# The first batch's token products wait for their own weights alone

## The chip, the cores and the metric

One Trainium2 chip, one core. The time is device microseconds of one execution. The kernel before takes 833.06 us (median of 3 runs, 832.63 to 834.16).

## The reference

Four batches, 576 tokens, 8 heads of 64. Three stages follow each other:

```
attention:  scores = q k^T / 8; keep a row's 32 largest; softmax; times v
gate:       x2 = (sigmoid(conv(x)) * (x @ w_val)) @ w_out
mixer:      theta = x2 @ w_theta;  zr, zi = x2 cos(theta), x2 sin(theta)
            y[t] = sum_s w_tok_r[t,s] zr[s] + w_tok_i[t,s] zi[s];  u = x2 + y
            out = u + max(u @ w_ch, 0)
```

A batch's gate and mixer need all heads of that batch's attention. Nothing passes from one batch to another. The result is float32 throughout.

## The kernel before

**Attention.** The scores' rows are cut into 144 tiles of 128 rows (36 a batch). A loop runs one iteration per tile, and in it each engine gets the pieces of several tiles at different stages: TensorE the scores of a tile three ahead (`ps`, L558 and L559), ScalarE their eviction (L572), VectorE the search for the 32 largest (L594 to L621) and the mask (L674), TensorE the transposes of the masked tile (`pt`, L687), ScalarE their eviction (L706), and at the end of a group of tiles TensorE the product with v (`px`, L778). In this text, tile k's *step* is the stretch from VectorE's mask of tile k to that of tile k+1; VectorE, ScalarE and the others take their queues strictly as the program lays them out, so a step's length is the pace of the whole loop.

**Gate and mixer** are two generators per batch, `front(b)` and `back(b)`, in the list `jobs`. In each iteration `work` draws from the first generator until a budget of about 4150 ns (less what attention's own TensorE work takes) is spent. A generator that yields "sync" ends the drawing for that iteration. These are waits of the program that writes the instructions, not of the chip: what they hold back is laid into a later iteration. So a "sync" sets where in each engine's queue the instructions stand.

`front(b)` lays the products with w_val (`pval`), w_out (`px2t`) and w_theta (`pth`), then sine and cosine (ScalarE, L202, which loads another table and the exponential's table again), and VectorE's products `z` (L986). `back(b)` lays

- the token products `py` (L1127): 4 chunks of channels by 2 halves of tokens (256 and 320 columns), each of 9 matmuls, 4 on `z_0` (the first 256 tokens) and 5 on `z_1` (the rest). VectorE adds a finished one to x2 (L1106, `y_out`);
- the channel products `ph` (L529) of u, which is split into a high and a low part (`U`: ScalarE L411, VectorE L415), with w_ch split likewise (`want`, `hi_-1`, `lo_-1`); VectorE adds them (L1158);
- the turned output `po` (L1180), ScalarE's copy (L1171) and the store.

**Weights** come as raw 64-bit words and are made into float32 by `cvt`, piece by piece, one piece begun every second iteration, in the order conv, val, out, theta, tok, ch. Each piece takes two ScalarE, three VectorE and one GpSimd instruction (L329, L332, L340, L341, L335, L354). `lacking[name]` counts what is still missing. `back(b)` begins when nothing is missing any more (L1114). `want(b, "ch", m)` (L466) splits w_ch up to chunk m; it is called from `y_out` after the second and fourth token product of the first half (L1110), and it also sends the parts to DRAM on SyncE's queue, for later batches. For batches 1 to 3 it does nothing in `back`, and nothing is lacking by then.

PE's queue is put in order by a list scheduler when the program is built; VectorE's and ScalarE's are as the loop writes them.

Of the kernel before, what the change touches and what calls it, by code (L numbers as in the profile page):

```python
# [90 lines left out]
def mixer(ctx, tc, qT, kT, vt, w_val, conv_t, w_out, w_theta, w_tok, w_ch, out, flag):  # L91
# [99 lines left out]
    taken, lacking = set(), {}  # L191
# [206 lines left out]
    def chunk(b, x, what, c):  # L398
        both = parts_of(b, x, what)
        w = COLS[x][1] - COLS[x][0]  # L400
        return both[:, 0, c, :w], both[:, 1, c, :w]
# [6 lines left out]
    def halve(hi, lo, src, key, also=None):  # L408

        def higher():  # L410
            nc.scalar.copy(hi, src)  # L411
            later.append(lower)

        def lower():
            engine(key).tensor_tensor(lo, src, hi.bitcast(F32), ALU.subtract)  # L415
            if also is not None:
                also()
            if PATIENT and attending[0]:
                later.append(lambda: done.add(key))
            else:  # L420
                done.add(key)

        mid.append(higher)

    def halve_room(b, x, what, src):

        both = parts_of(b, x, what)
        lo, hi = COLS[x]
        for c in range(0, NC, 2):
            halve(both[:, 0, c : c + 2, : hi - lo], both[:, 1, c : c + 2, : hi - lo], src[:, c : c + 2, lo:hi],  # L430
                  (what, b, c, x))
        if what == "L" and x:
            halve(both[:, 0, :, hi - lo :], both[:, 1, :, hi - lo :], src[:, :, NF * P :], (what, b, "last", x))

    def halved(b, x, what):
        return [(what, b, c, x) for c in range(0, NC, 2)] + [(what, b, "last", x)] * (what == "L" and x)
# [7 lines left out]
    def place(k, m):  # L444

        if k < 3 or k % 3 == 2:
            dt = F32R if k < 3 else I32
            both = []
            for t in ("hi", "lo"):
                if (t, m) in (("lo", 0), ("lo", 1)):  # L450
                    both.append(ml.tile([P, DM], dt, tag=f"{t}{m}", name=f"{t}{m}_{k}"))
                    continue
                pair = f"{t}{m - m % 2}{m - m % 2 + 1}"
                if (pair, k) not in places:
                    places[pair, k] = ml.tile([P, 2, DM], dt, tag=pair, name=f"{pair}_{k}")
                both.append(places[pair, k][:, m % 2, :])
            return both
        if (k, 0) not in places:
            names = ("val", "out") if k % 3 == 0 else ("theta", "ch")
            for t in range(2):  # L460
                places[k, t] = cp.tile([P, NC, DM], I32, tag=f"w_{names[t]}", name=f"w{t}_{k}")
        return [places[k, t][:, m, :] for t in range(2)]
# [3 lines left out]
    def want(b, name, last=NC - 1):  # L466

        k = PHASES.index((b, name)) if b else -1
        if k > 2:
            return  # L470
        for m in range(last + 1):
            if (b, name, m) in mats:
                continue
            src = W[name][:, m, :] if name == "theta" else W[name][:, :, m * P : (m + 1) * P]
            both = place(k, m)
            mats[b, name, m] = both
            stored[name, m] = dp.tile([P, 2, DM], I32, name=f"{name}{m}")

            def store(both=both, to=stored[name, m]):
                for t in range(2):  # L480
                    nc.sync.dma_start(to[:, t, :], both[t].bitcast(I32))

            hi, lo = (t if name == "theta" else t.rearrange("p (c w) -> p c w", c=NC) for t in both)
            halve(hi, lo, src, ("w", b, name, m), store)
# [11 lines left out]
    def used(b, name):  # L496

        if b:
            k = PHASES.index((b, name))
            for k in {0: (), 1: (3,), 2: (4, 5)}.get(k, (k + 3,)):  # L500
                bring(k)

    def mat(b, name, m, c):
        return tuple(t[:, c * P : (c + 1) * P] for t in mats[b, name, m])
# [7 lines left out]
    def after(*keys):  # L512
        while not done.issuperset(keys):
            yield "sync"
# [6 lines left out]
    def products(ps, terms):  # L521

        last, w = len(terms) - 1, ps.shape[-1]
        for i, (a, b) in enumerate(terms):
            ways = passes(a, b)
            for k, (x, y) in enumerate(ways):
                n = x.shape[-1]
                for o in range(0, P, n):
                    nc.tensor.matmul(ps[o : o + n], x, y, start=(i + k == 0),  # L529
                                     stop=(i == last and k == len(ways) - 1), skip_group_check=(n < P))  # L530
            owe[0] += w * (1.275 if len(ways) > 1 else 1.675)
            if owe[0] >= GRAIN and i < last:
                yield paid()
# [3 lines left out]
    def paid():  # L537
        ns, owe[0] = owe[0], 0.0
        return ns
# [181 lines left out]
    def close(part):  # L721
# [89 lines left out]
        if hp == NP - 1:  # L811
            jobs.append(front(b, (x,) if split else (0, 1)))
            if x:
                jobs.append(back(b))
# [284 lines left out]
    def back(b):  # L1099
        x2T = ms.pop(b)  # L1100

        def y_out(m, h, ps):
            lo, hi = COLS[h]

            def f():
                nc.vector.tensor_tensor(x2T[:, m, lo:hi], ps, x2T[:, m, lo:hi], ALU.add)  # L1106
                if m == NC - 1 and (h or b == B - 1):
                    for k in (h,) if b == B - 1 else range(2):
                        halve_room(b, k, "U", x2T)
                if not h and m % 2:  # L1110
                    want(b, "ch", m)
            return f

        while any(lacking.values()):  # L1114
            yield "sync"
        if b < B - 1:
            for h, m in [(h, m) for h in range(2) for m in range(NC)]:
# [36 lines left out]
        def h_out(m, h, ps):  # L1154
            lo, hi = COLS[h]

            def f():
                nc.vector.scalar_tensor_tensor(x2T[:, m, lo:hi], ps, 0.0, x2T[:, m, lo:hi], ALU.max, ALU.add)  # L1158
                n = b + 1
                if h and n in THREE:  # L1160
                    if m % 2:
                        want(n, "val", m)
                    if (n * NP + m, 0) in there:
                        split_x(n, m, 0)
                done.add(("o", b, m, h))
            return f
# [8 lines left out]
        def turned(tiles):  # L1175
            for i in tiles:
                w = P if i < NF else REM
                po = ps_m.tile([P, NC, P], F32, tag="m", name=f"po_{b}_{i}")
                for c in range(NC):
                    nc.tensor.transpose(po[:w, c, :], x2T[:, c, i * P : i * P + w], ident)  # L1180
                later.append(store(i, w, po))
                yield 450

        for h, m in [(h, m) for h in range(2) for m in range(NC)]:
            lo, hi = COLS[h]
            yield from after(*halved(b, h, "U"), ("w", b, "ch", m))
            ps = ps_m.tile([P, hi - lo], F32, tag="m", name=f"ph_{b}_{m}_{h}")
            yield from products(ps, [(mat(b, "ch", m, c), chunk(b, h, "U", c)) for c in range(NC)])
            later.append(h_out(m, h, ps))
            if (h, m) == (1, NC - 1):  # L1190
                used(b, "ch")
            yield paid()
            if h and m == 1:
                yield from after(*[("o", b, c, 0) for c in range(NC)])
                yield from turned([0, 1])
# [222 lines left out]
```

## Time and profile before

| | us |
|---|---|
| median of 3 runs | 833.06 |
| the profiled execution | 829.74 |
| its span, first to last instruction | 827.9 |

| engine | busy us | share of the span |
|---|---|---|
| TensorE (PE) | 725.3 | 88% |
| VectorE (DVE) | 669.0 | 81% |
| ScalarE (ACT) | 634.0 | 77% |
| GpSimd (POOL) | 451.7 | 55% |

The mean granted clock of TensorE is 0.958 of full speed. The shares are averages over attention with mixer work beside it (to about 711 us) and the last batch's mixer alone (from there on). How the engines stand in the stretch around the change is read from the rows below.

### The profile page before, as it was taken

How to read it: one execution, taken by the hardware profiler on the slowest of the kernel's cores; microseconds unless marked ns; L12 is line 12 of the kernel's file. 1: busy time of each engine (PE TensorE's matmuls, PEld its weight loads, DVE VectorE, ACT ScalarE, POOL GpSimd, SP SyncE). 2: the span in 40 equal slices, each digit the busy share in tenths (PEclk: the TensorE clock that was granted, in tenths of full speed). 3: DMA queues.
4: the chain of work that ended last, by engine and by line, in shares of the span. 5: the costliest groups of instructions: out<-in, count | busy, mean ns of one | idle time of the engine just before them, and what ended most of it. 6: DMA issues, size and time to landing. Idle time of an engine off the chain costs nothing.

```text
span 827.9 us, 15411 instructions
## 1 busy us (share of the span) xinstructions
PE 725.3 (88%) x4478; PEld 584.6 (71%) x4478; DVE 669.0 (81%) x2708; ACT 634.0 (77%) x1517; POOL 451.7 (55%) x557
## 2 busy tenths in 40 slices
PE   5467799958995799989889989999999899999995
PEld 3346577635754586778778767778988777898895
DVE  5999999879976979799899979989998695363522
ACT  6788999889769768788988988889987785346511
POOL 5976777446644554546687625647896252005500
PEclk9998999979997699989998999999999999999998
DMA  5676776545342225234855543234763200071002
GB/s 151 167 186 168 197 175 171 136 110 139 97 133 47 71 81 145 53 83 135 230 170 160 163 133 86 46 85 126 189 172 109 103 7 10 1 223 39 2 1 62
DMA packets 69985, 94.33 MB, mean 114 GB/s; under 512 B 13315, under 2 KB 36739, under 8 KB 69891
## 3 DMA queue, kind: packets, MB, share of 16 engines
q1 hardware_dynamic: 69568, 92.82, 41.2%
q8 instruction: 38, 0.62, 0.3%
q14 instruction: 59, 0.46, 0.2%
q10 hardware_dynamic: 320, 0.43, 0.2%
HBM read 49.96 MB, written 13.11 MB: 76 GB/s over the span
## 4 chain that ended last, share of the span: by engine, by line
PE 47%; DVE 27%; ACT 15%; POOL 4%; issue 3%; DMA 2%; SPq 1%; ACTq 0%; POOLq 0%; DVEq 0%
PE py L1127 9%; PE px L778 8%; DVE cand L594 5%; PE ph L529 4%; DVE s L674 4%; DVE thrs L621 4%; PE px2t L529 4%; PE pval L529 4%; PE pth L529 4%; PE pt L687 3%; PE py L1146 3%; PE ps L558 3%; ACT n L607 2%; DVE cand L600 2%; DVE gp L843 2%
## 5 line engine op out<-in xcount | busy, mean ns | idle before, releaser
L615 POOL TENSOR_TENSOR y<-s,n 128x576 f32<-128x576 f32 x144 | 188.9, 1312 | 205.0 <-DVE thrs L621 144.0
L594 DVE MAX8 cand<-s 128x8 f32<-128x96 f32 x864 | 210.5, 244 | 0.8 <-ACT s L572 0.6
L674 DVE SCALAR_TENSOR_TENSOR s<-s,thrs,e 128x576 f32<-128x576 f32 x144 | 137.8, 957 | 10.9 <-ACT e L202 10.9
L607 ACT ACTIVATE n<-s,tops 128x576 bf16<-128x576 f32 x144 | 112.1, 778 | 32.3 <-POOL y L615 11.3
L572 ACT ACTIVATE s<-ps 128x256 f32<-128x256 f32 (+1 forms) x288 | 103.7, 406 | 33.5 <-PE ps L691 11.5
L1127 PE MATMUL py<-w_tok,z 128*128 128x256 f32 (+1 forms) x432 | 115.0, 407 | 3.4 <-DVE z L986 3.4
L687 PE MATMUL pt<-ident,s 128*128 128x128 f32 x576 | 95.8, 290 | 25.3 <-ACT pT L706 17.3
L621 DVE MAX8 thrs<-y 128x8 f32<-128x584 f32 x144 | 109.3, 759 | 4.1 <-POOL y L616 3.6
L202 ACT ACTIVATE e<-s,least 128x576 f32<-128x576 f32 x144 | 110.8, 769 | 0.5 <-DVE s L674 0.4
L687 PEld LDWEIGHTS pt<-ident,s 128*128 128x128 f32 x576 | 70.5, 148 | 49.9 <-ACT pT L706 21.9
L558 PE MATMUL ps<-kh_None,q 128*128 128x256 f32 x240 | 93.7, 397 | 5.9 <-ACT s L572 3.9
L1127 PEld LDWEIGHTS py<-w_tok,z 128*128 128x128 f32 x432 | 77.8, 190 | 22.3 <-DVE z L986 5.0
L706 ACT COPY pT<-pt 128x512 f32<-128x512 f32 x128 | 73.2, 572 | 25.8 <-PE pt L687 15.6
L778 PE MATMUL px<-pT,v 128*64 128x256 f32 (+1 forms) x512 | 75.3, 430 | 17.3 <-ACT pT L706 17.3
L598 DVE MAX8 tops<-cand 128x8 f32<-128x48 f32 x432 | 82.8, 192 | 0.1
L559 PE MATMUL ps<-kl_None,q 128*128 128x256 f32 x240 | 72.5, 305 | 0.0
L778 PEld LDWEIGHTS px<-pT,v 128*64 128x64 f32 x512 | 34.1, 142 | 47.2 <-ACT pT L706 19.7
L558 PEld LDWEIGHTS ps<-kh_None,q 128*128 128x128 f32 x240 | 47.4, 198 | 22.2 <-ACT s L572 10.7
L600 DVE MATCH_REPLACE8 cand<-tops,cand 128x48 f32<-128x48 f32 x288 | 55.2, 192 | 0.0
L558 PE MATMUL ps<-kh,q 128*128 128x256 f32 (+1 forms) x80 | 36.0, 458 | 21.4 <-ACT s L572 9.3
L559 PEld LDWEIGHTS ps<-kl_None,q 128*128 128x128 f32 x240 | 48.1, 200 | 2.7 <-issue 0.5
L695 ACT COPY pT<-ps 64x128 f32<-64x128 f32 (+1 forms) x160 | 39.2, 245 | 11.5 <-PE ps L691 5.6
(206 smaller groups left out, 1726.9 us busy)
## 6 DMA issues: line engine op xcount, KB each, us to landing
kh_None<-kh_None SPq DMA_DIRECT2D x48, 144.0 KB, 2.7
kl_None<-kl_None SPq DMA_DIRECT2D x48, 144.0 KB, 2.7
v<-in_vt_dram SPq DMA_DIRECT2D x20, 256.0 KB, 3.3
out_dram<-x2T SPq DMA_DIRECT2D x16, 256.0 KB, 3.0
w<-ch SPq DMA_DIRECT2D x16, 256.0 KB, 4.6
w<-theta SPq DMA_DIRECT2D x16, 256.0 KB, 5.4
raw_hi<-in_w_tok_dram SPq DMA_DIRECT2D x7, 512.0 KB, 4.0
kh<-kh SPq DMA_DIRECT2D x24, 144.0 KB, 2.4
```

Source lines behind the costliest of these rows:

```text
L202: ins = nc.scalar.activation(out, src, func, **more).ins
L529: nc.tensor.matmul(ps[o : o + n], x, y, start=(i + k == 0), stop=(i == last and k == len(ways) - 1), skip_group_check=(n < P))
L558: nc.tensor.matmul(bank[:, :w], q2, kh[:, lo:hi], start=(j == js[0]), stop=False)
L559: nc.tensor.matmul(bank[:, :w], q2, kl[:, lo:hi], start=False, stop=(j == js[-1]))
L594: nc.vector.max(d["cand"][:, k, 8 * x : 8 * x + 8], s_tiles[i][:, x * SUB : (x + 1) * SUB])
L607: nc.scalar.activation(n, s_tiles[i], AF.Sign, bias=d["tops"][:, k, KC - 1 : KC], scale=-(1.0 + 2.0 ** -22), accum_out=acc)
L615: nc.gpsimd.tensor_tensor(y[:, :S], s_tiles[i], d.pop(("n", k)), ALU.mult)
L621: nc.vector.max(thrs[:, N - 1 - i : N - 1 - i + NK], d.pop(("y", k)))
L674: nc.vector.scalar_tensor_tensor(p, p, thr(i), e.exp, ALU.is_ge, ALU.mult, accum_out=part["sums"][:, e.slot : e.slot + 1])
L687: nc.tensor.transpose(e.pt[:, c, :], p[:, c * P : (c + 1) * P], ident)
L778: nc.tensor.matmul(px[d, :], of_v, pT[:, k, :], start=(c == 0), stop=(c == NF), skip_group_check=True)
L1127: nc.tensor.matmul(ps, z[:, m * P : (m + 1) * P], W["tok"][:, w, lo:hi], start=(i + k == 0), stop=(i == NF))
```

## The change

`back(b)` waits only until the token weights are converted. The second and third hunk split w_ch later: `y_out` notes each chunk of the first half in `due`, and calls `want` for all noted ones when its chunk is odd and w_ch is converted; whatever is left over is split before the channel products.

```diff
@@ back(b)
-                if not h and m % 2:
-                    want(b, "ch", m)
+                if not h:
+                    due.append(m)
+                    while due and m % 2 and not lacking["ch"]:
+                        want(b, "ch", due.pop(0))
             return f
 
-        while any(lacking.values()):
+        due = []
+        while lacking["tok"]:
             yield "sync"
@@ before the channel products
+        while lacking["ch"]:
+            yield "sync"
+        while due:
+            want(b, "ch", due.pop(0))
```

What this does to the queues. In the names below, `pt_51` are the transposes of tile 51, `py_0_1_0` is the token product of batch 0, channel chunk 1, token half 0; `z_0_0` and `z_0_1` are batch 0's z of the first 256 tokens and of the rest.

TensorE's queue from the transposes of tile 51 to those of tile 52, before:

```order
L687 MATMUL pt_51_3465<-ident_91,s_51_2911 128x128 x4
L558 MATMUL ps_60_0_3414<-kh1_6_None_3062,q21_88 128x256
L559 MATMUL ps_60_0_3414<-kl1_6_None_3063,q21_88 128x256
L691 MATMUL ps_60_0_3414<-ident_91,s_50_2844 64x128
L558 MATMUL ps_60_256_3418<-kh1_6_None_3062,q21_88 128x320
L559 MATMUL ps_60_256_3418<-kl1_6_None_3063,q21_88 128x320
L687 MATMUL pt_52_3508<-ident_91,s_52_2964 128x128 x4
```

The same place now, with the four matmuls ahead of it:

```order
L1130 MATMUL py_0_0_0_3421<-w_tok_138,z_0_1_3050 128x256 x4
L687 MATMUL pt_51_3470<-ident_91,s_51_2911 128x128 x4
L1130 MATMUL py_0_1_0_3493<-w_tok_138,z_0_0_2006 128x256 x2
L558 MATMUL ps_60_0_3414<-kh1_6_None_3062,q21_88 128x256
L559 MATMUL ps_60_0_3414<-kl1_6_None_3063,q21_88 128x256
L691 MATMUL ps_60_0_3414<-ident_91,s_50_2844 64x128
L558 MATMUL ps_60_256_3418<-kh1_6_None_3062,q21_88 128x320
L559 MATMUL ps_60_256_3418<-kl1_6_None_3063,q21_88 128x320
L1130 MATMUL py_0_1_0_3493<-w_tok_138,z_0_0_2006 128x256 x2
L1130 MATMUL py_0_1_0_3493<-w_tok_138,z_0_1_3050 128x256
L687 MATMUL pt_52_3523<-ident_91,s_52_2964 128x128 x4
L1130 MATMUL py_0_1_0_3493<-w_tok_138,z_0_1_3050 128x256 x2
```

Four token matmuls stand ahead of tile 51's transposes, five between them and tile 52's, two right behind these; before, none. The first four of all stand ahead of tile 50's transposes, and 23 ahead of tile 53's; before, the first one stood behind tile 54's.

TensorE's queue where batch 0's turned output ends, before:

```order
L687 MATMUL pt_76_4975<-ident_91,s_76_4375 128x128 x4
L1180 MATMUL po_0_2_4993<-ident_91,x2T_0_1697 128x128 x4
L1180 MATMUL po_0_3_5005<-ident_91,x2T_0_1697 128x128 x4
L687 MATMUL pt_77_5041<-ident_91,s_77_4424 128x128 x3
L558 MATMUL ps_86_0_4998<-kh1_9_None_4663,q21_88 128x256
L559 MATMUL ps_86_0_4998<-kl1_9_None_4664,q21_88 128x256
L691 MATMUL ps_86_0_4998<-ident_91,s_76_4375 64x128
L558 MATMUL ps_86_256_5002<-kh1_9_None_4663,q21_88 128x320
L559 MATMUL ps_86_256_5002<-kl1_9_None_4664,q21_88 128x320
L687 MATMUL pt_77_5041<-ident_91,s_77_4424 128x128
L1180 MATMUL po_0_4_5066<-ident_91,x2T_0_1697 64x128 x4
L529 MATMUL pval_1_0_0_5131<-X_1_0_4781,hi01_0_4831 128x256 x2
```

Now:

```order
L687 MATMUL pt_72_4801<-ident_91,s_72_4184 128x128 x3
L1183 MATMUL po_0_4_4826<-ident_91,x2T_0_1697 64x128 x4
L558 MATMUL ps_82_0_4831<-kh0_9_None_4536,q20_87 128x256
L559 MATMUL ps_82_0_4831<-kl0_9_None_4537,q20_87 128x256
L691 MATMUL ps_82_0_4831<-ident_91,s_72_4184 64x128
L735 MATMUL ps_82_0_4831<-ident_91,rs_7_1_4725 5x128
L558 MATMUL ps_82_256_4836<-kh0_9_None_4536,q20_87 128x320
L559 MATMUL ps_82_256_4836<-kl0_9_None_4537,q20_87 128x320
L778 MATMUL px_7_1_4839<-pT_7_1_4282,v2_7_0_4532 64x320 x8
L778 MATMUL px_7_1_4839<-pT_7_1_4282,v_last_121 64x320 x2
L687 MATMUL pt_73_4871<-ident_91,s_73_4242 128x128 x4
L558 MATMUL ps_83_0_4886<-kh0_9_None_4536,q20_87 128x256
```

The last turned output `po_0_4` stands with tile 72's transposes and not with tile 77's. The first three `pval` of batch 1 begin behind tile 74's transposes (before, tile 77's) and end, as before, ahead of the fourth's place behind tile 80's. From tile 80's transposes on TensorE's queue, and from tile 82's mask and exponential on VectorE's and ScalarE's, the instructions are the same in the same order in both programs. On GpSimd's queue the four low parts of x's second half for batch 1 (`X_1`, L415) stand one tile earlier, together with the last one of the first half (`X_0`).

VectorE's queue from the mask of tile 59, before:

```order
L674 SCALAR_TENSOR_TENSOR s_59_3396,sums_6_0_3559<-s_59_3396,thrs_127,e_59_3783 128x576
L796 TENSOR_TENSOR xT_5_3536<-px_5_1_3651,rb_5_1_3565 128x320
L415 TENSOR_TENSOR lo0_-1_3799<-w_ch_139,hi01_-1_3798 128x512
L415 TENSOR_TENSOR lo1_-1_3801<-w_ch_139,hi01_-1_3798 128x512
L621 MAX thrs_127<-y_62_3828 128x8
```

Now:

```order
L674 SCALAR_TENSOR_TENSOR s_59_3396,sums_6_0_3583<-s_59_3396,thrs_127,e_59_3807 128x576
L796 TENSOR_TENSOR xT_5_3560<-px_5_1_3676,rb_5_1_3589 128x320
L415 TENSOR_TENSOR lo0_-1_3823<-w_ch_139,hi01_-1_3822 128x512
L415 TENSOR_TENSOR lo1_-1_3825<-w_ch_139,hi01_-1_3822 128x512
L415 TENSOR_TENSOR lo23_-1_3828<-w_ch_139,hi23_-1_3827 128x512 x2
L621 MAX thrs_127<-y_62_3854 128x8
```

The four low parts of w_ch (and on ScalarE the four high parts ahead of them) stand in one place; before, the second pair stood three tiles later.

## Rows read from the trace of the kernel before

**Rows 1.** The page: its first line.
```profile
span 827.9 us, 15411 instructions
```

**Rows 2.** Busy time by stretch, all engines: stretch, its length, busy us (x instructions), granted clock, DMA.
```profile
core 0: us, PE busy (x) PEld busy (x) DVE busy (x) ACT busy (x) POOL busy (x), PEclk, DMA share, GB/s
188.10:206.70 18.60, 15.34 (x88) 10.37 (x86) 18.60 (x90) 17.74 (x46) 12.36 (x15) 0.91 0.56 154
253.90:281.90 28.00, 13.32 (x58) 8.86 (x60) 22.41 (x81) 22.92 (x50) 14.85 (x17) 0.60 0.16 34
259.40:283.20 23.80, 12.51 (x45) 7.89 (x47) 19.80 (x66) 18.75 (x42) 12.70 (x14) 0.50 0.22 46
263.86:279.03 15.17, 8.34 (x28) 5.46 (x28) 15.13 (x47) 11.45 (x28) 6.76 (x8) 0.50 0.16 35
281.90:390.55 108.65, 103.13 (x647) 83.79 (x644) 96.93 (x428) 86.09 (x215) 57.52 (x70) 0.96 0.38 103
281.90:401.95 120.05, 112.00 (x704) 92.11 (x700) 106.98 (x465) 97.41 (x242) 66.32 (x80) 0.95 0.43 116
283.30:300.00 16.70, 16.70 (x109) 13.52 (x106) 13.03 (x68) 12.63 (x33) 7.02 (x10) 1.00 0.37 96
```

**Rows 3.** The same view, line L674 alone: VectorE's masks, two instructions each.
```profile
0.00:253.90 253.90, 44.96 (x100) 0.95 0.57 149
188.10:206.70 18.60, 4.12 (x10) 0.91 0.56 154
281.90:390.55 108.65, 21.76 (x48) 0.96 0.38 103
```

**Rows 4.** Timeline of TensorE: start, us, instruction, [idle before <- what ended it].
```profile
255.70 0.31 PE L559 MATMUL ps<-kl_None,q 128*128 128x320 f32 x1
263.86 1.12 PE L687 MATMUL pt<-ident,s 128*128 128x128 f32 x4 [7.85 <-ACT pT L706]
...
268.41 1.12 PE L687 MATMUL pt<-ident,s 128*128 128x128 f32 x4 [1.84 <-ACT pT L703]
...
279.03 1.12 PE L778 MATMUL px<-pT,v 128*64 128x256 f32 x4 [3.94 <-ACT pT L706]
```

**Rows 5.** Timeline of VectorE, same stretch: the products with cosine and sine.
```profile
264.45 2.48 DVE L986 TENSOR_TENSOR z<-px,z 128x512 f32<-128x512 f32 x4
...
274.04 0.66 DVE L986 TENSOR_TENSOR z<-px,z 128x512 f32<-128x512 f32 x1
```

**Rows 6.** Timeline of ScalarE, same stretch.
```profile
276.98 0.78 ACT L607 ACTIVATE n<-s,tops 128x576 bf16<-128x576 f32 x1 [3.66 <-POOL y L616]
```

**Rows 7.** The chain that ended last, token products: start, us, what, two records a matmul.
```profile
286.42 3.89 PE py L1127 x18
...
343.67 3.23 PE py L1127 x12
```

**Rows 8.** Waits of VectorE from 282 to 402 us: total us, times, longest.
```profile
DVE x2T L1106 <- PE py L1127: 8.1, 4, 3.3
DVE lo_-1_3799 L415 <- ACT hi_-1_3798 L411: 1.7, 1, 1.7
```

**Rows 9.** Timeline of VectorE, 289 to 360 us: additions of token products, pile-up.
```profile
290.34 0.42 DVE L1106 TENSOR_TENSOR x2T<-py,x2T 128x256 f32<-128x256 f32 x1 [1.04 <-PE py L1127]
...
299.48 0.42 DVE L1106 TENSOR_TENSOR x2T<-py,x2T 128x256 f32<-128x256 f32 x1 [2.62 <-PE py L1127]
...
341.79 0.49 DVE L1106 TENSOR_TENSOR x2T<-py,x2T 128x320 f32<-128x320 f32 x1 [3.34 <-PE py L1127]
...
353.62 2.68 DVE L843 SCALAR_TENSOR_TENSOR gp<-xT,w_conv,gp 128x576 f32<-128x576 f32 x2
...
356.30 2.73 DVE L415 TENSOR_TENSOR U<-x2T,U 128x512 fp32r<-128x512 f32 x4
```

**Rows 10.** Timeline of TensorE, 352 to 358 us: the first channel products.
```profile
357.01 0.58 PE L529 MATMUL ph<-U,hi_-1_3798 128*128 128x256 f32 x1 [1.26 <-DVE U L415]
```

**Rows 11.** Timeline of GpSimd, 403 to 406 us.
```profile
403.73 1.70 POOL L415 TENSOR_TENSOR X<-xT,X 128x320 fp32r<-128x320 f32 x2
```

## The prediction

> **What bounds the kernel now.** I read the page first, then the busy time by stretch, then the timelines of the stretch in which the change works, and last VectorE's waits behind it.
>
> The span is 827.9 us [rows 1]. Fifty masks lie ahead of 253.90 us (100 instructions, two a mask) [rows 3], so tile 50's step begins there. Steps 50 to 53 fill 28.00 us, 7.00 each, and in them TensorE is busy for 13.32 us only, at a mean granted clock of 0.60 [rows 2]. This is a hole. ScalarE does batch 0's last sines and cosines with two table loads, and TensorE stands from about 256.0 to 263.86 us because the evicted transposes are late [rows 4]; then VectorE makes `z`, five products up to 274.7 us [rows 5], and is busy for 15.13 of 15.17 us [rows 2]. So the hole belongs to ScalarE and VectorE, not to TensorE: work put on TensorE there costs nothing as long as it is done in time, and its absence shortens nothing.
>
> Behind it lie 24 steps (54 to 77) in 108.65 us [rows 2, 3], 4.53 each, with batch 0's token products, channel products and turned output beside attention. TensorE is busy for 103.13 us of them, VectorE for 96.93: the two share the bound. Where attention runs nearly alone, as in steps 36 to 40, five masks take 18.60 us, 3.72 each, and VectorE is busy all the time [rows 2, 3]. A step without mixer work is thus 0.81 us shorter. From 281.90 to 401.95 us VectorE idles 120.05 - 106.98 = 13.07 us [rows 2]; 8.1 of that it waits for token products, at the head of its queue [rows 8].
>
> **What is moved.** 23 of batch 0's 72 token matmuls stand ahead of tile 53's transposes now, and before none did. One with 256 columns takes 3.89 / 9 = 0.432 us, one with 320 3.23 / 6 = 0.538 (two records a matmul) [rows 7]. So 9.9 us of TensorE's work, out of 36 x 0.432 + 36 x 0.538 = 34.9, go into the hole. The back of batch 0 ends five tiles earlier (72 instead of 77). From tile 80 on nothing can move further ahead, since batch 1's gate waits for its own attention; what is won must be won before.
>
> **Does it fit?** Between 263.86 and 279.03 us TensorE did 8.34 us of its own work, all of it at the clock's low level, 0.50 (1.2 GHz) [rows 2]. The four matmuls on `z_0` ahead of tile 50's transposes run while it would stand. The other 19 come behind the first `z`, at 265 us at the earliest [rows 5]. I take the low level up to tile 51's transposes: four matmuls at 0.864 = 3.5 us from about 266.6, so these begin near 270.0, not at 268.41 [rows 4]. From there TensorE has some 5.6 us of own work (at the low level) and 15 matmuls. At the high level that is 2.8 + 15 x 0.432 = 9.3 us, done at 279.3, just where the product with v begins now (279.03) [rows 4]. The 1.6 us of delay are covered by ScalarE, which stands for 3.66 us before 276.98 [rows 6]. I cost the hole at nothing but VectorE's addition of the first product, 0.42 us [rows 9], which came later before.
> Bounds: all 19 at the high level, and TensorE is early, with no gain since VectorE is full; all 19 at the low level, 16.4 + 8.34 = 24.8 us in 15.17, and it is 9.6 us late.
>
> The clock decides this, and the row shows it at 0.50 for the whole of 259.40 to 283.20 us, with TensorE busy for 12.51 of 23.80, and at 1.00 from 283.30 us on, after it had worked without a pause since 279.03 [rows 2, 4]. The Trainium skill (TensorE: Matmul & The Clock Gate, "What's actually happening") says that the low clock is the default state and that sustained activity releases it. By that rule the added matmuls, which close the pauses, lift the clock inside the hole, and the sum is the one above; by the row alone, which holds no such activity in the hole, it stays low and the case "late" below comes true.
>
> **The sum, in two ways.** First by the pace of steps: 20 steps (54 to 73) keep 4.53 us, since 25.0 us of token products in 20 are about as dense as 34.9 in 24; four (74 to 77), with three `pval` alone, fall to 3.72. 4 x 0.81 = 3.2 us, less 0.42: 2.8.
> Second by VectorE's waits: the two for products of the first half, 1.04 and 2.62 [rows 9], go, as these are done in the hole. In step 70 two conv taps (2.68 us) and the four low parts of u (2.73) pile up, and TensorE waits 1.26 us for the latter [rows 9, 10]; now u is split four tiles earlier, away from the taps. 1.04 + 2.62 + 1.26 - 0.42 = 4.5 us. The long wait of 3.34 for a product of 320 columns stays, as these run beside attention as densely as before.
> Smaller edits: w_ch's four parts are split in one go; VectorE waited 1.7 us for the first pair before [rows 8] and waits in that one place for both now: nothing. The eight stores stand in one row on SyncE's queue ahead of the next head's loads, four of them not there before; they wait for two more low parts, about 0.7 us each by the four of u [rows 9]. The scores that need these loads stand behind tile 62's transposes, three tiles on: nothing. GpSimd's five splits of x stand together; four took 3.4 us [rows 11]; VectorE may wait for one more, 0.85 us.
> I take 4.2 us, nearer the second sum, as VectorE's queue carries the loop's pace, and expect it to be kept to the end, since the order is the same from tile 82 on. Profiled execution: 829.74 - 4.2 = 825.5 us. It ran 3.3 us below the median of the runs, so for the median 833.06 - 4.2 = 828.9.
>
> **Rivals.**
> - *More:* the work done in the hole unloads TensorE so far that VectorE waits no more between 281.90 and 401.95 us, but for the 1.7 us for ScalarE's split of w_ch [rows 8]: 13.07 - 1.7 - 0.42 = 10.9 us, 822.2. For it: TensorE is the busier of the two in steps 54 to 77. Against: the products of 320 columns meet the same density of work as before. With the 1.7 us too it would be 820.4.
> - *Nothing:* VectorE and ScalarE carry steps 54 to 79 whatever TensorE does, or what was won until 73 is given back where batch 1's x is split: GpSimd's five splits hold up VectorE's search, and the gate's first products wait there in both programs. Left: 3.66 of the waits, less 0.42 and less some 2.2 us at these splits (by estimate the 1.26 us that TensorE waited for u's split, and one split of 0.85): 1.1 us, 832.0. For it: VectorE is busy for 96.93 of 108.65 us. Against: the 3.72 us of a step without mixer work.
> - *Late:* the clock stays low in the hole. The token matmuls stand ahead of the transposes in TensorE's queue, which takes them in order; 9.6 us late less the 3.66 that ScalarE can spare, less the 4.2 won later: +1.7, without ScalarE's slack +5.4. The middle, 836.6. It decides from 7.9 us of delay on, that is when some 15 of the 19 run at the low level. For it: 0.50 over the whole hole. Against: the pauses in it are closed.
> - *Not what it says:* that w_ch's conversion ends so soon after the token weights' that nothing moves is excluded by the order, which shows five tiles.
>
> **Chances.** Forecast 0.58 (its own range 825.5 to 831.4, a gain of 1.7 to 7.5), more 0.14, nothing 0.17, late 0.11. What a measurement of this kernel can tell from no change is 0.2%, 1.7 us. Faster by more: the forecast but for a small share, and "more", together 0.72; within: "nothing" and that share, 0.18; slower 0.10. The range that leaves out 2 in 10 goes from 822.0, just below "more", to 832.8, which takes in "nothing" and leaves out "late".
>
> **What would show it.** Token matmuls between 256 and 279 us; granted clock back at 1.00 before 275 us; steps 50 to 53 still about 28 us; tile 54's mask within 1 us of 281.97; the first two waits of VectorE for token products gone, a long one at a 320-column product left; steps 74 to 77 below 4 us; masks from tile 82 to the end in the same distances as before. Wrong it would be if steps 50 to 53 grew by more than 3 us, if steps 54 to 73 took over 4.7 us each, or if the lead at tile 80 were lost later.

## The result and the profile after

The changed kernel takes 822.0 us in the first measurement (median of 4 runs, 821.0 to 824.7) and 823.5 in a second one beside other kernels (6 runs, 821.6 to 825.2). The ratio to the kernel before is 0.988 (95% interval 0.984 to 0.992) and 0.990 (0.988 to 0.993): faster, by 8 to 10 us. The forecast was 828.9, a gain of 4.2. Sign and place were right, and the size was about half of what came. The 822.0 of the first measurement stands on the lower end of the stated range (822.0 to 832.8).

The page of the changed kernel, the span and the busy time of each engine:

```profile
span 819.2 us, 15413 instructions
...
PE 717.9 (88%) x4478; PEld 577.3 (70%) x4478; DVE 667.2 (81%) x2708; ACT 633.8 (77%) x1517; POOL 453.3 (55%) x557
```

The span was 827.9 [rows 1], so 8.7 us went. TensorE's busy time fell by 7.4 us from 725.3 although it does the same products; the mean granted clock is 0.973, before 0.958, so less of them ran at the low level. The change reaches the steps from tile 50 to tile 81. Their two ends are these masks, first before, then now:

```profile
253.95 0.81 DVE L674 SCALAR_TENSOR_TENSOR s<-s,thrs,e 128x576 f32<-128x576 f32 x1
...
411.45 0.80 DVE L674 SCALAR_TENSOR_TENSOR s<-s,thrs,e 128x576 f32<-128x576 f32 x1
```

```profile
253.65 0.81 DVE L674 SCALAR_TENSOR_TENSOR s<-s,thrs,e 128x576 f32<-128x576 f32 x1
...
403.38 0.81 DVE L674 SCALAR_TENSOR_TENSOR s<-s,thrs,e 128x576 f32<-128x576 f32 x1
```

They took 157.50 us and take 149.73, so 7.8 us of the gain stand here; a second trace of the changed kernel has 149.73 as well. Where in them the time went, the stretches tell. Steps 50 to 53, then 54 to 73, 74 to 77 and 78 to 81 of the changed kernel, and behind them the two parts of the hole on either side of the clock's return:

```profile
core 0: us, PE busy (x) PEld busy (x) DVE busy (x) ACT busy (x) POOL busy (x), PEclk, DMA share, GB/s
253.65:282.02 28.37, 20.81 (x118) 16.20 (x116) 22.78 (x82) 22.95 (x50) 14.95 (x17) 0.88 0.18 38
282.02:368.89 86.87, 82.44 (x539) 65.68 (x535) 83.56 (x363) 76.13 (x191) 50.17 (x61) 1.00 0.48 127
368.89:383.03 14.14, 10.49 (x86) 9.74 (x82) 14.14 (x67) 13.78 (x38) 9.84 (x12) 1.00 0.81 235
383.03:403.35 20.32, 13.71 (x88) 10.28 (x89) 16.38 (x73) 15.65 (x39) 14.21 (x23) 0.83 0.40 100
```

```profile
259.96:266.78 6.82, 3.17 (x11) 2.66 (x12) 3.71 (x8) 6.79 (x14) 2.75 (x3) 0.50 0.64 136
266.78:282.02 15.24, 13.86 (x81) 10.49 (x80) 15.20 (x56) 9.88 (x25) 8.52 (x10) 1.00 0.04 8
```

The same steps of the kernel before (54 to 73, 74 to 77, 78 to 81), cut at its own masks:

```profile
281.97:373.75 91.78, 86.26 (x521) 69.04 (x518) 80.21 (x356) 71.70 (x178) 47.03 (x58) 0.96 0.37 98
373.75:390.63 16.88, 16.88 (x129) 14.82 (x128) 16.74 (x74) 14.40 (x38) 10.50 (x13) 1.00 0.43 131
390.63:411.41 20.78, 17.04 (x121) 14.96 (x120) 18.49 (x75) 19.41 (x48) 16.41 (x25) 0.92 0.93 245
```

Steps 50 to 53 are as long as before (28.37 against 28.00 [rows 2]), with 7.5 us more of TensorE in them. Steps 54 to 73 lose 4.9 us and 74 to 77 lose 2.7. Over these 24, VectorE was busy for 96.93 of 108.65 us [rows 2]; now it is for 83.56 + 14.14 = 97.70 of 101.01. The same work stands closer together, and VectorE is busy for 97%. In all, from mask 50 on: +0.35 in the hole, -4.9, -2.7, -0.5 in steps 78 to 81, -0.6 to the end, and the rest (0.3) was there before the change's place. The 0.6 are not the change's: they go in steps 110 to 130, and the two traces of one later version differ by as much there (29.09 and 29.71 us in steps 110 to 115).

TensorE's timeline in the hole, the added matmuls among the work of before [rows 4]:

```profile
255.55 1.89 PE L1130 MATMUL py<-w_tok,z 128*128 128x256 f32 x8
263.56 1.12 PE L687 MATMUL pt<-ident,s 128*128 128x128 f32 x4 [6.12 <-ACT pT L706]
...
266.07 2.25 PE L1130 MATMUL py<-w_tok,z 128*128 128x256 f32 x8
268.15 0.62 PE L687 MATMUL pt<-ident,s 128*128 128x128 f32 x4
...
274.47 0.70 PE L1130 MATMUL py<-w_tok,z 128*128 128x256 f32 x2 [1.33 <-DVE z L986]
...
275.75 3.18 PE L1130 MATMUL py<-w_tok,z 128*128 128x256 f32 x14
278.87 0.65 PE L778 MATMUL px<-pT,v 128*64 128x256 f32 x4
```

Transposes took 1.12 us at 263.56 and 0.62 at 268.15: the clock came back between them. VectorE's waits from 282 to 403 us (total, times, longest), which answer to [rows 8]:

```profile
DVE gp L843 <- POOL gp L835: 3.9, 1, 3.9
DVE lo_-1_3823 L415 <- ACT hi_-1_3822 L411: 1.7, 1, 1.7
DVE x2T L1106 <- PE py L1130: 1.0, 1, 1.0
DVE xT L796 <- ACT rb L757: 0.6, 1, 0.6
```

Of the 8.1 us of waits for token products 1.0 is left. The wait of 3.9 us for GpSimd was 1.3 in the kernel before:

```profile
DVE gp L843 <- POOL gp L835: 1.3, 1, 1.3
```

### The profile page after: what moved, and what is told of

Read it like the earlier page. It is cut to its first block, busy times and chain, and to the rows that moved or that the text cites. A ratio compares the mean times of both kernels' runs of the same rounds, so it can differ in the third digit from the quotient of the medians.

```text
span 819.2 us, 15413 instructions
## 1 busy us (share of the span) xinstructions
PE 717.9 (88%) x4478; PEld 577.3 (70%) x4478; DVE 667.2 (81%) x2708; ACT 633.8 (77%) x1517; POOL 453.3 (55%) x557
## 4 chain that ended last, share of the span: by engine, by line
DVE 40%; PE 39%; ACT 9%; POOL 7%; issue 2%; DMA 2%; SPq 0%; ACTq 0%; POOLq 0%; DVEq 0%
DVE cand L594 8%; PE py L1130 7%; DVE s L674 7%; DVE thrs L621 6%; PE px L778 6%; PE px2t L529 4%; PE pval L529 4%; PE pth L529 4%; DVE cand L600 3%; PE ph L529 3%; DVE tops L598 3%; PE py L1149 3%; PE pt L687 3%; DVE gp L843 3%; PE ps L558 2%
## 5 line engine op out<-in xcount | busy, mean ns | idle before, releaser
L674 DVE SCALAR_TENSOR_TENSOR s<-s,thrs,e 128x576 f32<-128x576 f32 x144 | 138.0, 959 | 10.9 <-ACT e L202 10.9
L558 PE MATMUL ps<-kh_None,q 128*128 128x256 f32 x240 | 91.5, 388 | 6.3 <-ACT s L572 3.0
```

Source lines behind the costliest of these rows:

```text
L558: nc.tensor.matmul(bank[:, :w], q2, kh[:, lo:hi], start=(j == js[0]), stop=False)
L674: nc.vector.scalar_tensor_tensor(p, p, thr(i), e.exp, ALU.is_ge, ALU.mult, accum_out=part["sums"][:, e.slot : e.slot + 1])
```

## The experiments

All are timed against the kernel before on their own chip. Three theories: LOAD, what TensorE does in the hole it doesn't do in steps 54 to 77, whose bound it was; CLOCK, the clock's early return helps behind the hole; PILE-UP, VectorE's and ScalarE's pieces of batch 0 stand at better places.

The times scatter by some us within each kernel. Between the masks of tile 50 and tile 82 the traces are far steadier (the two of the changed kernel agree to 0.01 us; most others have one trace), so that stretch is given beside the times; "by the trace" means it.

| trace | us from tile 50's mask to tile 82's | against before |
|---|---|---|
| before | 157.50 | |
| changed kernel, two traces | 149.73, 149.73 | -7.8 |
| nine matmuls ahead | 155.36 | -2.1 |
| hole filled | 155.98 | -1.5 |
| w_ch split in one place | 157.87 | +0.4 |
| twenty left out | 152.53 | -5.0 |
| load put back | 155.81 | -1.7 |
| left out and filled | 153.18 | -4.3 |
| one matmul less | 152.51 | -5.0 |
| u split one tile later | 151.17 | -6.3 |
| splits of x parted, two traces | 147.75, 147.74 | -9.8 |
| two chunks at a time, on top | 148.27 | -9.2 |

**Nine matmuls ahead instead of 23** (against the changed kernel):

```diff
-        while lacking["tok"]:
+        while lacking["tok"] or lacking["ch"] > 1:
```

> The changed kernel, but batch 0's token products start only when the token weights are there and at most one piece of w_ch is missing. 9 token matmuls stand ahead of tile 53's transposes instead of 23, and batch 0's turned output ends with tile 76's transposes, not 72's (before: 0, and 77's). Theory LOAD (TensorE was the bound in steps 54 to 77, the hole is free, so what leaves that stretch is gained nearly one to one: 8 of 9.9 us): 9 x 0.432 = 3.9 us moved, gain about 3.2 us, 829.7. Theory CLOCK (the gain is the clock that stays up): the pauses are half closed, gain of 1 to 4 us. Theory PILE-UP (the gain is that conv taps and u's split, and w_ch's two splits, no longer stand in each other's way): the order behind is nearly that of before, gain under 1 us.

829.2 us, ratio 0.9965 (0.994 to 0.999): 2.9 us gained, by the trace 2.1. Nine matmuls are 3.9 us of TensorE's work, so 0.75 us were won for each us moved, by the trace 0.55. LOAD and CLOCK both allowed this; PILE-UP's "under 1 us" missed.

**The hole filled, nothing moved** (against the kernel before; 23 matmuls whose sums nobody reads):

```diff
+        if b == 0:
+            while lacking["tok"]:
+                yield "sync"
+            ...  # 23 token matmuls on z_0 and z_1 into a spare tile
         while any(lacking.values()):
```

> The kernel before, with 23 token matmuls added in the hole (the same as those that the change moves there, into scratch tiles that nobody reads); batch 0's own 72 stay behind tile 53's transposes. LOAD: no gain, 0 to 0.5 us slower, 833. CLOCK: the clock is back before 270 us as in the changed kernel, and the product with v at 279 us runs at the high level: 2.1 us faster there, more if the lead holds, 829 to 831. PILE-UP: no gain.

829.2 us, 0.997 (0.994 to 1.000): some 2.5 us. Its hole is 28.00 us long, so filling it costs nothing, and the clock there is that of the changed kernel (0.88). The hole and steps 54 to 77:

```profile
254.40:282.40 28.00, 20.42 (x114) 16.31 (x114) 22.39 (x81) 22.94 (x50) 14.83 (x17) 0.88 0.16 35
282.40:390.00 107.60, 102.37 (x644) 83.22 (x641) 96.51 (x429) 87.13 (x216) 57.00 (x70) 0.97 0.39 105
```

The filling alone is thus worth about a quarter of the gain by the middle of its interval (0.3 to 4.7 us), and a fifth by the trace (1.5 of 7.8). That is what CLOCK expected; LOAD's "no gain" missed. TensorE stays the busier one in steps 54 to 77 (102.37 of 107.60).

**w_ch split in one place** (the kernel before; at `m == 3`, as the change does):

```diff
-                if not h and m % 2:
+                if not h and m == NC - 1:
```

> The kernel before, with w_ch's four parts split in one place, after the fourth token product of the first half; the start of the token products is as before. LOAD and CLOCK: 0 within 0.5 us. PILE-UP: one stop instead of two for VectorE (1.7 and 0.6 us of waits before), 1 to 2 us faster, 831 to 832.

832.2 us, 1.0011 (0.999 to 1.003): nothing, and by the trace 0.4 us more. This part of PILE-UP falls.

**Twenty matmuls left out, none moved into the hole** (the kernel before):

```diff
-                for x in range(2):
+                for x in range(1 if b == 0 and h == 0 else 2):
...  # the sum of such a product ends with z_0's last matmul
```

> The kernel before, leaving out 20 of batch 0's token matmuls (those of the first half of tokens on the later 320 tokens' z); the start is as before, nothing runs in the hole, 52 matmuls stand in steps 54 to 63, and from the channel products on the order is that of the changed kernel. LOAD: as fast as the changed kernel within 1.5 us, 821 to 824, since only the dense stretch counts. CLOCK: the hole keeps its low clock to 283 us, so 2 us or more slower than the changed kernel. If work in the hole has a price of its own, this one is faster than the changed kernel by that price.

827.2 us, 0.993 (0.991 to 0.995): 5.7 us for 8.6 us of TensorE's work, with the clock low through the hole and beyond it:

```profile
258.40:285.70 27.30, 14.37 (x53) 8.59 (x53) 21.69 (x80) 22.05 (x49) 14.69 (x17) 0.50 0.25 54
```

That is slower than LOAD had it (821 to 824) and as CLOCK had it (2 us or more behind the changed kernel). Less load without CLOCK, but with the earlier places that batch 0's later pieces get by it, carries more than half by the middle of its interval (3.8 to 7.7 us), and 5.0 of 7.8 us by the trace.

**The changed kernel again.** No edit.

> The changed kernel itself, on the chip of the three kernels beside it, since its time so far comes from 4 runs (821.0 to 824.7). Both theories: 820.5 to 824.5 us against 832.1 for the kernel before. Above 826 the gain would be nearer the 4.2 us forecast than the 10 measured, and the question of the second half would be gone.

823.5 us, told above. The gain stands.

**The load put back** (against the changed kernel; 16 matmuls run twice, 8.6 us; the other engines' queues are the same, row for row):

```diff
-                            nc.tensor.matmul(ps, z[:, m * P : (m + 1) * P], W["tok"][:, w, lo:hi],
-                                             start=(i + k == 0), stop=(i == NF))
+                            for r in range(2 if b == 0 and h == 1 and x == 0 else 1):
+                                nc.tensor.matmul(ps, z[:, m * P : (m + 1) * P], W["tok"][:, w, lo:hi],
+                                                 start=(i + k + r == 0), stop=(i == NF))
```

> The changed kernel with the work that it took off steps 54 to 77 put back on TensorE alone: the four matmuls on z_0 of each of batch 0's four 320-column products run twice (16 more matmuls of 0.54 us, 8.6 us, against 20 x 0.43 = 8.6 taken off); the output isn't the reference's. VectorE, ScalarE and GpSimd have the same instructions in the same order, and the hole keeps its 23 token matmuls. Theory LOAD (TensorE was the bound of these steps): VectorE waits for the 320-column products again, some 5.7 us of the gain go, 826 to 829 us. Rival ORDER (what counts is when VectorE and the others get batch 0's pieces, and the clock's return in the hole): under 2 us more than the changed kernel, 822 to 824.

830.1 us, 0.997 (0.996 to 0.999): 6.6 us more than the changed kernel on the same chip (5.8 by the ratios, 6.1 by the trace), somewhat more than LOAD had it, and ORDER falls. What is left of the gain, with the clock's return, the new places and 1.3 us of load not put back, is 1.7 us by the trace. VectorE's waits from 282 to 403 us show where:

```profile
DVE xT L796 <- ACT rb L757: 4.1, 1, 4.1
DVE gp L843 <- POOL gp L835: 3.9, 1, 3.9
DVE x2T L1106 <- PE py L1131: 3.4, 3, 1.9
```

The waits for token products are back (3.4), and one of 4.1 us for ScalarE's copy of what TensorE makes in its queue behind them. These 16 matmuls stand in steps 59 to 65 and the moved ones stood from step 55 on, so 6.1 may be an upper end; no run shows it.

**Twenty left out and the hole filled**: the two edits above together.

```diff
+        ...  # the 23 matmuls in the hole
-                for x in range(2):
+                for x in range(1 if b == 0 and h == 0 else 2):
```

> The kernel before without 20 of batch 0's token matmuls and with 23 matmuls in the hole whose sums nobody reads: the two edits measured apart (5.0 and 2.9 us by the medians), now together; the output isn't the reference's. Theory SUM (the change is these two effects, which add): 823 to 825.5 us, near the changed kernel. Rival OVERLAP (a faster clock in the hole helps only because TensorE is late behind it, so with the load gone it buys nothing): 826.5 to 828.5, as with the matmuls left out alone.

827.2 us, 0.994 (0.992 to 0.996): no faster than without the filling, as OVERLAP had it. But the two runs differ by more than the filling. On ScalarE's queue w_ch's and u's high parts and the first pieces of batch 1's x and w_val stand later here. From tile 54's mask to tile 64's this run takes 42.99 us, the one without the filling 45.49: the filling wins 2.5 us with the load gone, and they are lost behind, where the queues differ. So it isn't shown that the clock is no second term beside LOAD. By the trace 3.4 us of the gain had no owner here. Beside the 3.9 us for GpSimd that the changed kernel has too, VectorE waits longest for the last 320-column product. TensorE's timeline there, then VectorE's:

```profile
327.30 3.40 PE L1150 MATMUL py<-w_tok,z 128*128 128x320 f32 x12
...
331.39 2.37 PE L778 MATMUL px<-pT,v 128*64 128x320 f32 x16
333.59 0.71 PE L778 MATMUL px<-pT,v_last 128*64 128x320 f32 x4
334.23 0.66 PE L687 MATMUL pt<-ident,s 128*128 128x128 f32 x4
334.72 0.70 PE L1150 MATMUL py<-w_tok,z 128*128 128x320 f32 x2
```

```profile
335.46 0.49 DVE L1106 TENSOR_TENSOR x2T<-py,x2T 128x320 f32<-128x320 f32 x1 [3.70 <-PE py L1150]
```

The last matmul (two records) stands behind the product with v and a tile's transposes; in the changed kernel the whole product stands ahead of them.

**One matmul less**, this one, on top of the two edits above:

```diff
+                            last = (b, h, m) == (0, 1, NC - 1)
+                            if not (last and i == NF):
                                 nc.tensor.matmul(...
```

> As the matmuls left out and the hole filled, and besides without the last matmul of batch 0's last 320-column product, so 21 are left out. In the run before, this one matmul stood behind the 20 of the product with v and a tile's transposes in TensorE's queue, and VectorE's addition waited 3.70 us for it at the head of its own. Theory PLACE (what the changed kernel has beyond the lower load is that this product ends ahead of the product with v): the wait falls to some 0.5 us and the time by 2.5 to 3.2 us, to 824 to 825 us, near the changed kernel. Rival LOAD ALONE (one matmul less is 0.54 us of TensorE, and VectorE waits elsewhere instead): 826.5 to 827.2 us.

826.2 us, 0.993 (0.991 to 0.995), the same within its interval and 0.7 us less by the trace; between PLACE and LOAD ALONE, nearer the latter. PLACE falls in this form: the wait for the product is gone, and in the next step VectorE waits 3.03 us for ScalarE's high parts of u. ScalarE's timeline shows why, first here, then in the changed kernel:

```profile
332.67 0.77 ACT L202 ACTIVATE e<-s,least 128x576 f32<-128x576 f32 x1
335.46 0.59 ACT L706 COPY pT<-pt 128x512 f32<-128x512 f32 x1 [2.02 <-PE pt L687]
...
338.12 2.40 ACT L411 CAST U<-x2T 128x512 fp32r<-128x512 f32 x4
```

```profile
330.98 0.77 ACT L202 ACTIVATE e<-s,least 128x576 f32<-128x576 f32 x1
331.65 2.38 ACT L411 CAST U<-x2T 128x512 fp32r<-128x512 f32 x4
333.94 0.57 ACT L706 COPY pT<-pt 128x512 f32<-128x512 f32 x1
```

The changed kernel has u's split one tile earlier in ScalarE's queue, beside the product with v, where ScalarE stands for 2.02 us in the other.

**u split one tile later** (the changed kernel; ScalarE's queue around it is then that of the run above):

```diff
-                if m == NC - 1 and (h or b == B - 1):
+                if m == NC - 1 and (h and b or b == B - 1):
...
+        if b == 0:
+            yield "sync"
+            for k in range(2):
+                later.append(lambda k=k: halve_room(b, k, "U", x2T))
         while lacking["ch"]:
```

> The changed kernel with batch 0's split of u one tile later: on ScalarE the four high parts (L411, 2.4 us) now stand behind the eviction of the transposes that TensorE makes after a group's product with v (3.1 us of TensorE), where the two runs with matmuls left out have them; in the changed kernel they stand ahead of that eviction. All arithmetic and TensorE's load stay. The run with one matmul less moved VectorE's wait from the product to these high parts (3.03 us) and won nothing, so Theory SLOT: what the changed kernel has beyond the lower load is that ScalarE splits u beside the product with v instead of standing, and VectorE's search goes on; one tile later it loses 2 to 3.5 us, 825 to 826.7 against 823.1 (10 runs of the changed kernel). Rival ELSEWHERE (the rest of the gain comes from other steps, as the move of w_ch's four parts behind a lighter load): within 1 us, 822 to 824.

824.3 us, 0.990 (0.988 to 0.993): 1.2 above the 10 runs of the changed kernel by medians, and nothing by the ratios. By the trace it is 1.4 us. That is between the two expectations. The first pieces of batch 1's x and w_val stand later on ScalarE's queue too, so not all of it need be u's. The stall of ScalarE is there, but VectorE waits only 0.90 us for u:

```profile
334.39 0.59 ACT L706 COPY pT<-pt 128x512 f32<-128x512 f32 x1 [2.02 <-PE pt L687]
```

SLOT is worth up to some 1.4 us; in the size expected of it, it fell.

**GpSimd's five splits of x parted** (against the changed kernel, in batch 1's gate):

```diff
+                if b == 1 and (x, c) == (0, NC - 1):
+                    yield "sync"
```

> The changed kernel with a yield between GpSimd's split of X_0 and of X_1 in batch 1's gate, so that its five splits no longer stand in one row and VectorE's tap (3.9 us of waiting at 391.5 us) finds GpSimd done. Theory GIVEN BACK (the 2.3 us lost from step 79 to 80 come from this row): the wait falls below 1 us and the time is 1.5 to 2.5 us under the changed kernel, 819.5 to 820.5. Rival WAIT MOVES (the products with w_val need both splits, and VectorE waits there or for the scores): the same within 1 us, 821 to 823.

820.2 us, 0.986 (0.984 to 0.989).

> The changed kernel with the yield between the splits of X_0 and X_1 once more, for a time on the chip of the next kernel and a second sample, as the first had 6 runs. Theory GIVEN BACK, kept by the first sample: 819.5 to 821.5 us against some 832.5 for the kernel before, 2 to 3 us under the changed kernel. Rival WAIT MOVES: 822 to 823.5.

819.8 us, 0.986 (0.983 to 0.989). Both samples are 3 us below the changed kernel (medians 820.2 of 12 runs and 823.1 of 10); by the trace the edit wins 2.0. GIVEN BACK is right. VectorE's tap and GpSimd's product for it in the changed kernel, then the product, a split and the tap in this one:

```profile
391.52 1.67 DVE L843 SCALAR_TENSOR_TENSOR gp<-xT,w_conv,gp 128x576 f32<-128x576 f32 x2 [3.90 <-POOL gp L835]
```

```profile
390.09 1.40 POOL L835 TENSOR_TENSOR gp<-gp,ct 128x576 f32<-128x576 f32 x1
```

```profile
385.14 1.42 POOL L835 TENSOR_TENSOR gp<-gp,ct 128x576 f32<-128x576 f32 x1
...
388.44 2.78 POOL L415 TENSOR_TENSOR X<-xT,X 128x320 fp32r<-128x320 f32 x2
```

```profile
388.35 2.15 DVE L843 SCALAR_TENSOR_TENSOR gp<-xT,w_conv,gp 128x576 f32<-128x576 f32 x2
```

GpSimd's product now stands ahead of the four later splits, and the tap follows the mask without a pause. This version beats both kernels.

**The token products two chunks at a time**, on top of that, meant to put 8 matmuls instead of 4 ahead of tile 50's transposes:

```diff
+        if b == 0:
+            for h, ms2 in [(h, (m, m + 1)) for h in range(2) for m in range(0, NC, 2)]:
+                ...  # z_0's part of both chunks, then z_1's
```

> The yield of the kernel before in this list, and batch 0's token products two chunks at a time, the z_0 parts of both first: in the hole 8 matmuls stand ahead of tile 50's transposes instead of 4, while TensorE would stand, and the token products end one tile earlier. Theory LOAD (what TensorE does while it would stand unloads the steps behind): 0.5 to 1.5 us under the yield alone, 819 to 820. Rival FULL (VectorE is busy for 83.5 of 86.9 us of steps 54 to 73 already, and two products that end close together make it wait for neither): the same within 0.5 us, 820 to 821. If the additions of two products come at a bad place behind the product with v, 822 or more.

820.5 us, 0.986 (0.984 to 0.989): the same, and by the trace 0.5 us more. But the trace has the same 4 matmuls (8 records) ahead of tile 50's transposes, and 24 instead of 23 ahead of tile 53's. In steps 54 to 73 TensorE is busy for 82.54 us, without this edit for 82.44. So the edit moved next to nothing, and whether a still lighter TensorE buys anything while VectorE is 97% busy was not tested; FULL is not shown.

## Why the prediction was right in sign and short in size

**The hole costs nothing: right.** 0.35 us more, where 0.42 were priced. Tile 51's transposes were forecast at 270.0 and came at 268.15, the product with v at 279.3 and came at 278.87: the clock returned at 266.78, already in the first four matmuls behind `z`, not behind them. The row of before, 0.50 from 259.40 to 283.20 us [rows 2], was of a TensorE that paused; with the pauses closed it was 1.00. The Trainium skill (TensorE: Matmul & The Clock Gate, "What's actually happening") has the low clock as the default that activity releases, and the trace agrees: 0.50 from 259.96 to 266.78, 1.00 from there to 282.02. "Late" is refuted by this, and two runs with the hole filled have the same return.

**The pace of steps 54 to 73: the step that failed.** The prediction kept it at 4.53 us, "since 25.0 us of token products in 20 are about as dense as 34.9 in 24". They aren't: 25.0 / 20 = 1.25 us a step against 34.9 / 24 = 1.45, and 0.20 x 20 = 4.1 us of TensorE's work was dropped by that sentence. Measured: 86.87 / 20 = 4.34, that is 3.7 us less than 20 x 4.53, and 4.9 less than the 91.78 that these steps took before. Worked out otherwise, TensorE was busy for 103.13 of 108.65 us [rows 2] and had 9.9 taken off: 93.2, and 92.93 is what the trace has. That they meet is luck in part: 6.8 us of batch 1's products with w_val stand in these steps now, and the products with v and the channel products take 4.9 less there. Steps 54 to 77 went down by 7.65, or 0.77 us for each us taken off. The runs give a like price, by their ratios and by the trace: 0.75 and 0.55 (nine ahead), 0.66 and 0.58 (twenty left out), 0.54 and 0.50 (and filled), 0.68 and 0.71 (put back). At 0.50 to 0.75, 9.9 us are worth 5.0 to 7.4. The run that puts the load back is the cleanest, as the other engines' queues are those of the changed kernel.

**The long wait at a 320-column product: wrong.** It was to stay (3.34 us [rows 9]); the longest one left is 0.98. Its density argument was the same one. The first two waits went, as forecast.

**Steps 74 to 77: the pace right, the gain priced too high.** 14.14 / 4 = 3.54 against 3.72. But before they took 16.88 / 4 = 4.22 and not the mean of 4.53, so 2.7 us went and not 3.2.

**u's split away from the taps: not shown as a term.** The gap of 1.26 us [rows 10] is gone. Gone with it is a second stretch of low clock at that place: before, 0.50 from 354.90 to 361.73 us, in step 70; now 1.00 from 282.02 to 389.66. But the one test of u's place moves it by one tile, not back to the taps, and shows 1.4 us at most.

**Given back at the splits of x: the price was right, its case was not.** "Nothing" had 2.2 us lost there; from tile 79's mask to tile 80's the lead fell from 8.8 to 6.5. But 1.5 us came back two steps on, and the masks from tile 82 to 110 keep a lead of 8.0, that is the same distances as before, as forecast.

**The rival "More"** had the size (822.2) and nearly the mechanism: VectorE idled for 108.65 - 96.93 = 11.7 us in steps 54 to 77 [rows 2], and now for 101.01 - 97.70 = 3.3. What was against it in the prediction was the density again.

**What stays open.** Putting the load back takes 6.1 of the 7.8 us, and filling the hole alone wins 1.5, so the two terms nearly make up the gain. That they add is not shown, as the run with both edits has u split a tile later, and that alone may cost up to 1.4 us; the worth of the places of u's and x's splits stays open with it.

## What to carry to other kernels

Where an engine is at 95% of a stretch, count its work before and after in us, not as "about as dense": a small difference a step times twenty steps is the answer. Work moved into an engine's hole was worth here some 0.5 to 0.75 us for each us that it took off the place where it was. The next engine was then 97% busy, and what a further us would win was not tested. Time a change in the stretch that it reaches as well as over the whole, and look at the queues of both kernels before two runs are said to differ by one edit. Once a lead is won, look for the next row of instructions on a third engine that gives part of it back; parting one such row won another 2 to 3 us.

## What the runs showed of the hardware

VectorE's mask (L674, two inputs from the on-chip buffer) takes 0.80 us at 375.32 us, but took 2.01 at the head of step 77 of the changed kernel, beside GpSimd's two-input products. VectorE's rows, then GpSimd's:

```profile
375.32 0.80 DVE L674 SCALAR_TENSOR_TENSOR s<-s,thrs,e 128x576 f32<-128x576 f32 x1
...
378.37 2.01 DVE L674 SCALAR_TENSOR_TENSOR s<-s,thrs,e 128x576 f32<-128x576 f32 x1
...
383.03 1.33 DVE L674 SCALAR_TENSOR_TENSOR s<-s,thrs,e 128x576 f32<-128x576 f32 x1
```

```profile
378.37 1.40 POOL L253 TENSOR_TENSOR kl_None<-kl_None,kh_None 128x576 fp32r<-128x576 f32 x1
379.72 1.94 POOL L253 TENSOR_TENSOR ql_None<-ql_None,qh_None 128x576 fp32r<-128x576 f32 x1
...
383.02 2.07 POOL L415 TENSOR_TENSOR X<-xT,X 128x256 fp32r<-128x256 f32 x2
```

The mask and GpSimd's product begin together at 378.37; 1.40 + 0.80 = 2.2 is near the mask's 2.01, as if it ran behind the other. The Trainium skill (SBUF — State Buffer, "Who interferes with whom") says that a VectorE instruction with two inputs there and a GpSimd one that reads there block each other, and these rows agree. Step 77 is long (4.66 us) with no wait of VectorE in it, for this reason in part: the blocked time counts as busy. So it does in the 97% above.
